# Attention's second head is asked for in the bias stage from four buffers; three smaller moves in the order of narrowing and of the last rows

## The chip, the cores and the metric

The kernel runs on one core of a Trainium2 chip. The metric is the device time of one execution in microseconds (us). Before the change three timed runs took 439.25, 441.69 and 442.11 us: 441.69 in the median. One more execution was profiled; its rows are those read here.

The engines are named as the profile names them: PE multiplies matrices (PEld is its loading of weights), DVE and ACT are the two vector engines, POOL is GpSimd, and SP only issues DMA transfers. Each works through its own list of instructions in order and waits on semaphores for the others. POOL and ACT can issue transfers too.

## The reference

Three layers, one after the other. Attention has 2 batches (B), 8 heads (H), 576 positions (S) and 64 numbers per head; its bias is made by a small net with 32 hidden units. A mixture of 8 experts follows, with at most 288 tokens for each, and a gated block on all 1152 tokens.

```
scores = scale * np.matmul(q, k.transpose(0, 1, 3, 2))
x = (psi_rel / psi_i)[..., None]
bias = np.maximum(x @ w1 + b1, 0.0) @ w2          # 576 x 576 for each head
scores = scores + bias.transpose(2, 0, 1)[None]
attn = softmax(scores);  out = np.matmul(attn, v)
...
h = relu(einsum("ecd,edf->ecf", disp, w1));  y = einsum("ecf,efd->ecd", h, w2)
...
g = x @ w_gate;  val = x @ w_val
return (g * sigmoid(g) * val) @ w_out
```

## The kernel before

Nearly every operand is split into a high part (a rounded copy) and a low part (what the copy left), and a product is made of two or three. The splitting is work for DVE, ACT and POOL.

**Bias stage** (`bias_phase`). 36 steps, each for 16 rows of positions. A step makes four tiles r of 128 x 576 (L587 on DVE; in seven of nine steps one of the four is L585 on ACT), multiplies them with w2 on PE (L591), copies the product out on ACT (`leave`, L600) and writes it to DRAM (biasd, L601) from one of six buffers (be). The bias tiles of head 0 are read back by `bias` (L196 to L202). Between the steps the rows of head 0 are split: they were asked for at the start, and ACT and DVE do it (`hi="A"`, `L=V`).

**Loads.** `loader` gives `load(h, b)`: a transfer of q, k and v of a head and a batch (raw, 800 KB, L227), then six instructions that make the split operands QK, K2 and W. The transfer is issued at the first step of this generator. For heads 1 to 7 all six are POOL's, in order L238 (twice), L240, L242, L247, L249. The buffers raw come from a pool of two.

**Attention stage** (`attn_phase`). 72 steps u, nine for each head. A step issues the scores of the next u (L296 on PE), the sum with the bias and the maximum (L311, DVE), the exponential (L328, ACT), the transposes (L348) and the split of what comes back (L351 ACT, L367 and L373 DVE), and pieces of older work on PE: the products with v (L395) and the products that gather the heads (L422). In head h the rows of head h+1 are asked for: at its steps 0 and 4 for head 0 (`LOADS0`), at 0 and 5 for the others (`LOADS`). `inv` (L409, nine elements for each of 128 partitions) prepares the division of a head. The order on each engine is the order in which this code is written.

**Experts** (`experts`, `Experts.full`). The routing is computed in four pieces (`route`). Expert by expert, eight weight blocks of 512 KB are loaded (wr, L999 and L1002), split (L1008 ACT, L1009 DVE) and used (L1038, L1052). Among them `extra(k)` puts one further piece at a time: the last piece of the routing (small, few, late), and for the gated block the narrowing of its 64-bit weights. `narrow(f)` is four steps: L790 and L792 on DVE, L794 on ACT, L796 on DVE, which then issues the load `load64(f + 2)`. `Y0` is how many places of the first expert pass before `extra(0)` begins.

**Gated block** (`swiglu`, `block`). Twelve steps f; each has two products (`gate(f, 0)` and `gate(f, 1)`, L1290 on PE, two tiles of 304 tokens), the elementwise part (L1297 ACT, L1298 DVE), the split of its result (`parts`, L1302 ACT, L1303 DVE) and the product with w_out of the step before (`outp`, L1311). In between stand the pieces of narrow(f + 3) and of split(f + 1). At the end five blocks of rows (t = 0 to 4) are copied out (L1319 ACT, L1321 DVE) and sent by POOL (`put`, L1322). `M2` and `M3` say how many of the products of the last but one step stand before the second half's gate and how many are left to the loop over the last blocks.

## Time and profile before

| | us |
|---|---|
| median of three timed runs | 441.69 |
| the profiled execution, its own time | 440.11 |
| its span, to which all rows refer | 437.9 |
| bias stage | 0 to about 66 |
| attention | about 66 to 219 |
| routing and first expert | about 219 to 269 |
| second and third expert | about 269 to 302 |
| gated block | about 302 to 438 |

Within the span PE is busy for 90%, DVE for 79%, ACT for 62% and POOL for 30%. A row of a timeline gives the start, the time, the engine, the line, the operation, the tiles (out<-in) and how many instructions are merged into it; in square brackets stands the idle time of the engine before it and what ended it. A merged row's time runs from the start of the first to the end of the last.

### The profile page before, as it was taken

The numbers are of one execution on the slowest core, as the hardware profiler recorded it, in microseconds if no ns is written. First come the engines' busy times: TensorE is split into PE (matmuls) and PEld (weight loads), VectorE is DVE, ScalarE is ACT, GpSimd is POOL, SyncE is SP. The second block draws the span as 40 slices with busy tenths as digits, with TensorE's granted clock in tenths as the row PEclk, the third lists the DMA queues.
The fourth block names the chain that finished last, engine by engine and source line by source line (L and its number), as shares of the span: only waits on it lengthen the run. The fifth ranks groups of instructions, "written<-read, shape, count | busy, mean of one in ns | idle before, by whom it ended". The sixth has DMA issues, their size and how long they took to land.

```text
span 437.9 us, 8781 instructions
## 1 busy us (share of the span) xinstructions
PE 395.4 (90%) x3136; PEld 344.2 (79%) x3136; DVE 345.7 (79%) x747; ACT 270.9 (62%) x579; POOL 131.2 (30%) x122
## 2 busy tenths in 40 slices
PE   8786678579999999999999989997979999999994
PEld 4332226579999999999989979995968888888992
DVE  6999996469999999999778878944887777777341
ACT  4888787469989899899624367444354444444221
POOL 2000000798979999995200300000000000000003
PEclk9999899889999999999999999999999999999998
DMA  7555447782766857732194898983444444440003
GB/s 255 210 217 191 162 190 237 260 293 82 226 184 206 258 166 236 239 99 77 28 283 137 230 293 188 335 229 129 145 144 145 144 146 144 145 144 2 0 1 117
DMA packets 54017, 75.75 MB, mean 173 GB/s; under 512 B 16514, under 2 KB 35714, under 8 KB 53968
## 3 DMA queue, kind: packets, MB, share of 16 engines
q1 hardware_dynamic: 51744, 70.62, 50.9%
q10 hardware_dynamic: 1616, 2.62, 2.1%
q0 software_dynamic: 608, 1.89, 1.3%
q8 instruction: 26, 0.43, 0.4%
q14 instruction: 23, 0.19, 0.2%
HBM read 58.54 MB, written 16.59 MB: 172 GB/s over the span
## 4 chain that ended last, share of the span: by engine, by line
PE 42%; DVE 21%; ACT 10%; DMA 7%; issue 6%; POOL 2%; SPq 1%; DVEq 0%; ACTq 0%; POOLq 0%
PE pg L1290 9%; PE tp L348 5%; PE po L395 5%; PE sc L296 5%; DMA wr<-in_ew 4%; DVE swl L806 4%; DVE wf L792 4%; PE ph L1038 4%; PE pb L591 3%; PE po L422 3%; ACT pth L351 2%; PE etp L910 2%; DVE sg L1298 2%; ACT ex L328 2%; DMA bias<-biasd 2%
## 5 line engine op out<-in xcount | busy, mean ns | idle before, releaser
L311 DVE CUSTOM_DVE_ANT_0 ex<-sc,bias 128x576 f32<-128x576 f32 x72 | 53.9, 750 | 9.7 <-PE tt L358 7.4
L591 PE MATMUL pb<-r,w 128*32 128x288 f32 x576 | 45.3, 424 | 15.1 <-ACT r L585 9.3
L238 POOL TENSOR_TENSOR QK<-raw,zero 128x640 fp32r<-128x640 f32 x28 | 34.5, 1253 | 78.0 <-DVE mx L311 75.4
L587 DVE TENSOR_SCALAR r<-ltab,sl,nb 128x576 f32<-128x576 f32 x116 | 57.3, 592 | 0.3 <-PE pb L591 0.2
L328 ACT ACTIVATE ex<-ex,mx 128x576 f32<-128x576 f32 x72 | 55.8, 775 | 1.4 <-DVE mx L311 0.7
L351 ACT ACTIVATE pth<-tp 128x512 fp32r<-128x512 f32 (+1 forms) x80 | 43.7, 553 | 16.3 <-PE tp L348 8.3
L296 PE MATMUL sc<-QK 128*128 128x288 f32 x160 | 49.6, 326 | 3.8 <-POOL QK L240 3.4
L591 PEld LDWEIGHTS pb<-r,w 128*32 128x32 f32 x576 | 18.6, 112 | 41.4 <-ACT r L585 21.7
L367 DVE TENSOR_TENSOR ptl<-tp,pth 128x512 fp32r<-128x512 f32 (+1 forms) x80 | 49.7, 629 | 1.7 <-ACT pth L351 1.0
L1290 PE MATMUL pg<-x2h,swh 128*128 128x304 f32 x192 | 46.4, 309 | 4.9 <-DVE sg L1298 4.1
L348 PE MATMUL tp<-cst,ex 128*128 128x128 f32 x288 | 45.1, 280 | 5.3 <-DVE ptl L367 3.1
L1322 POOL DMA_INDIRECT out<-ob,ids x5 | 4.9, 973 | 146.3 <-ACT ob L1319 145.4
L296 PE MATMUL sc<-K,QK 128*128 128x288 f32 x160 | 45.4, 299 | 1.2 <-POOL K L242 1.2
L1290 PE MATMUL pg<-x2l,swh 128*128 128x304 f32 x192 | 43.9, 303 | 0.0
L395 PE MATMUL po<-pth,W 128*128 128x256 f32 (+1 forms) x145 | 43.7, 322 | 0.0
L1290 PE MATMUL pg<-x2h,swl 128*128 128x304 f32 x192 | 43.6, 301 | 0.0
L348 PEld LDWEIGHTS tp<-cst,ex 128*128 128x128 f32 x288 | 33.1, 143 | 9.9 <-ACT ex L328 4.6
L1302 ACT ACTIVATE sh<-sg 128x608 fp32r<-128x608 f32 (+1 forms) x13 | 8.8, 673 | 51.1 <-DVE sg L1298 51.1
L1290 PEld LDWEIGHTS pg<-x2h,swh 128*128 128x128 f32 x192 | 32.7, 188 | 9.7 <-DVE sg L1298 7.1
L1298 DVE TENSOR_TENSOR sg<-pg,sg 128x304 f32<-128x304 f32 x48 | 20.7, 469 | 22.1 <-PE pg L1290 18.7
L296 PEld LDWEIGHTS sc<-QK 128*128 128x128 f32 x160 | 30.6, 191 | 5.5 <-POOL QK L240 3.6
L395 PE MATMUL po<-ptl,W 128*128 128x256 f32 (+1 forms) x116 | 33.4, 309 | 0.0
(209 smaller groups left out, 1041.9 us busy)
## 6 DMA issues: line engine op xcount, KB each, us to landing
raw<-in_qkv SPq DMA_DIRECT2D x16, 800.0 KB, 7.2
biasd<-be SPq DMA_DIRECT2D x36, 288.0 KB, 2.1
wr<-in_ew SPq DMA_DIRECT2D x19, 512.0 KB, 9.0
w<-in_mwg SPq DMA_DIRECT2D x12, 512.0 KB, 3.6
w<-in_mwv SPq DMA_DIRECT2D x12, 512.0 KB, 4.9
w<-in_mwo SPq DMA_DIRECT2D x12, 512.0 KB, 6.6
bias<-biasd SPq DMA_DIRECT2D x16, 288.0 KB, 4.0
bias<-biasd SPq DMA_DIRECT2D x17, 256.0 KB, 4.2
```

The costliest lines, as they stand in the source:

```text
L238: P.tensor_tensor(QK[:, o:o + n], raw[:, o:o + n], view(zero, 0, (0, n)), op=ALU.add)
L296: nc.tensor.matmul(sc[:, c, :288], l, K[:, o + c * 288:o + (c + 1) * 288], start=n == 0, stop=n == len(lhs) - 1)
L311: V.tensor_tensor_reduce(e.rearrange("p (c j) -> p c j", c=2), sc[:, :, :288], head[h][:, t].rearrange("p (c j) -> p c j", c=2), scale=-0.125,
L328: A.activation(ex[u], ex[u], AF.Exp, bias=mx, scale=-1.0, accum_out=sums[h][:, col:col + 1])
L348: nc.tensor.transpose(x[:, kt], e[:, kt * 128:(kt + 1) * 128], ident)
L351: A.activation(hi[:, :4, c], x[:, :, o], AF.Copy)
L367: V.tensor_tensor(lo[:, :, c], x[:, :, o], hi[:, :4, c].bitcast(F32), op=ALU.subtract)
L395: nc.tensor.matmul(po[:, :w], W[:, kt], src[:, kt, a:a + w], start=k == 0, stop=k == 8)
L587: V.tensor_scalar(r[g], x, s, nb, op0=ALU.mult, op1=ALU.max)
L591: nc.tensor.matmul(pb[strips[g], c, :288], w2, r[g][:, c * 288:(c + 1) * 288], start=True, stop=True, skip_group_check=True,)
L1290: nc.tensor.matmul(g[:, :TB], w[:, a * 4 + kk], x[:, kk, c0 + b * TB:c0 + (b + 1) * TB], start=kk == 0 and i == 0, stop=kk == 3 and i == 2,)
L1298: V.tensor_tensor(sg[:, cs], g[:, :TB], sg[:, cs], op=ALU.mult)
```

## The change

Four things. (1) The transfers of head 1 (both batches) are issued in the bias stage, at its steps 12 and 16, instead of at attention's steps 0 and 4, and the pool for raw has four buffers instead of two. The staging tiles of `prepare` lie in the bias stage's own pool. (2) `Y0` is 4 instead of 3. (3) In the gated block's step 1 the last step of narrow(3) comes after `parts` instead of before the older product. (4) `M3` is 3 instead of 1. The gated block's code is built three more times for other numbers of kept tokens, in branches that this execution does not enter.

```diff
--- before.py
+++ after.py
@@ -46,9 +46,11 @@
 
 ONA = (1, 2, 3, 5, 6, 7, 8)
 L0, L1 = 20, 2
+LOADS0 = (12, 16)
 STEPS1 = 4
 
-LOADS0, LOADS = (0, 4), (0, 5)
+RAW = 4
+LOADS = (0, 5)
 SHARE, SHARE4 = 0.68, 0.0
 LAST = (2.0, 2.0, 2.0, 2.0)
 LATE = ((7, 0, 1), (7, 1, 0), (7, 1, 1))
@@ -57,11 +59,11 @@
 NSPL = 3
 Q1 = 3
 N2 = 3
-Y0, Y1 = 3, 5
+Y0, Y1 = 4, 5
 REGS, LATE_REGS = 2, 5
 PICK = 3
 
-M2, M3 = 2, 1
+M2, M3 = 2, 3
 
 WARM0 = 7
 WARM = (16, 24)
@@ -214,7 +216,7 @@
 def loader(tc, ctx, ins):
 
     nc = tc.nc
-    raw_p = ctx.enter_context(tc.tile_pool(name="araw", bufs=2))
+    raw_p = ctx.enter_context(tc.tile_pool(name="araw", bufs=RAW))
     qk_p = ctx.enter_context(tc.tile_pool(name="aqk", bufs=4))
     V, A, P = nc.vector, nc.scalar, nc.gpsimd
     one = ctx.enter_context(tc.tile_pool(name="az", bufs=1))
@@ -454,9 +456,8 @@
         u += 1
         if u < nu:
             h, b, t = seq[u]
-            at = LOADS if h else LOADS0
-            if h + 1 < H and u % 9 in at:
-                b = at.index(u % 9)
+            if 0 < h < H - 1 and u % 9 in LOADS:
+                b = LOADS.index(u % 9)
                 loads.append(load(h + 1, b))
                 qk[h + 1, b] = next(loads[-1])
             if h + 1 < H and 1 <= u % 9 <= NQ:
@@ -506,9 +507,9 @@
     return late[0]
 
 
-def prepare(nc, pool, ins, rt, tids):
-
-    zi = pool.tile([128, DM], F32, name="zi")
+def prepare(nc, pool, one, ins, rt, tids):
+
+    zi = one.tile([128, DM], F32, name="zi")
     nc.gpsimd.memset(zi, 0.0)
     zb = pool.tile([128, 12], F32, name="zb")
     nc.gpsimd.memset(zb, float(BIG))
@@ -545,7 +546,7 @@
     for b in range(B):
         loads.append(load(0, b, "A", V))
         qk[0, b] = next(loads[-1])
-    others = prepare(nc, one, ins, rt, tids)
+    others = prepare(nc, pool, one, ins, rt, tids)
     zi = next(others)
 
     warm = ps.tile([128, 512], F32, name="pb1", tag="T")
@@ -612,6 +613,10 @@
             bias(0, k // 8 - 1)
         if k in (20, 21, 22):
             next(others, None)
+        if k in LOADS0:
+            b = LOADS0.index(k)
+            loads.append(load(1, b))
+            qk[1, b] = next(loads[-1])
         if k >= L0 and (k - L0) % L1 == 0:
             next(loads[0], None)
             if STEPS1 > (k - L0) // L1:
@@ -1351,7 +1356,11 @@
             elif f == 1:
                 for _ in split(2, (0, 1)):
                     pass
-            for _ in nar if f else ():
+            if f == 1:
+
+                for _ in range(2):
+                    next(nar, None)
+            for _ in nar if f > 1 else ():
                 pass
             if f:
                 outp(f - 1, *prev, 0, mid)
@@ -1359,7 +1368,7 @@
             if f == 0:
                 po = banks("po", range(nt))
             parts(sg, sh, sl, 0, nb)
-            for _ in () if f else nar:
+            for _ in () if f > 1 else nar:
                 pass
             if f:
                 outp(f - 1, *prev, mid, nt)
```

On SP's queue, in the bias stage: rows of the kernel before (biasd are the writes of bias tiles, bias the reads of head 0's, raw the rows of a head).

```order
L601 DMA biasd_91<-be 128x576 x2
L202 DMA bias<-biasd_90 128x576
L601 DMA biasd_91<-be 128x576 x6
L601 DMA biasd_92<-be 128x576 x2
L199 DMA bias<-biasd_91 128x512
L200 DMA bias<-biasd_91 128x64
```

The same place now.

```order
L602 DMA biasd_91<-be 128x576 x2
L204 DMA bias<-biasd_90 128x576
L602 DMA biasd_91<-be 128x576 x2
L229 DMA raw<-in_qkv 128x1600
L602 DMA biasd_91<-be 128x576 x4
L229 DMA raw<-in_qkv 128x1600
L602 DMA biasd_92<-be 128x576 x2
L201 DMA bias<-biasd_91 128x512
```

Two transfers of rows stand between the writes; they stood behind the whole stage before. On POOL the order is unchanged: head 1's instructions are the first behind its memsets.

On DVE, in the first expert, behind the routing's small instructions (late is their last; wf and w are the narrowing, wl the split of an expert's weights, hl that of its hidden tiles): before.

```order
L754 CAST late<-small 1x3
L790 TENSOR_SCALAR wf_3175<-w_3178 128x1536
L1009 TENSOR_TENSOR wl_3204<-wr_3197,wh_3203 128x1024
L874 TENSOR_LOAD regs x2
L1413 BRANCH_PREFETCH_HINT
L1043 SCALAR_TENSOR_TENSOR hl<-ph,hh 128x288
L792 SCALAR_TENSOR_TENSOR wf_3175<-w_3178,wf_3175 128x1536
L1043 SCALAR_TENSOR_TENSOR hl<-ph,hh 128x288
L1009 TENSOR_TENSOR wl_3206<-wr_3198,wh_3205 128x1024
L1043 SCALAR_TENSOR_TENSOR hl<-ph,hh 128x288
L796 SCALAR_TENSOR_TENSOR wf_3175<-w_3178,wf_3175 128x1536
```

The same place now.

```order
L1014 TENSOR_TENSOR wl_3204<-wr_3197,wh_3203 128x1024
L879 TENSOR_LOAD regs x2
L1422 BRANCH_PREFETCH_HINT
L1048 SCALAR_TENSOR_TENSOR hl<-ph,hh 128x288
L748 TENSOR_TENSOR small<-list 128x2
...
L759 CAST late<-small 1x3
L795 TENSOR_SCALAR wf_3175<-w_3178 128x1536
L1048 SCALAR_TENSOR_TENSOR hl<-ph,hh 128x288
L797 SCALAR_TENSOR_TENSOR wf_3175<-w_3178,wf_3175 128x1536
L1014 TENSOR_TENSOR wl_3206<-wr_3198,wh_3205 128x1024
```

One split of weights (wl_3204) now stands ahead of the routing's last piece and of the narrowing.

On DVE, in the gated block's step 1 (swl is the split of its weights, sg the elementwise part, sl the split of the result): before.

```order
L806 TENSOR_TENSOR swl_3181<-wf_3177,swh_3180 128x512 x2
L792 SCALAR_TENSOR_TENSOR wf_4279<-w_3179,wf_4279 128x1536
L796 SCALAR_TENSOR_TENSOR wf_4279<-w_3179,wf_4279 128x1536
L1298 TENSOR_TENSOR sg<-pg,sg 128x304 x2
L1303 TENSOR_TENSOR sl<-sg,sh 128x608
```

The same place now.

```order
L811 TENSOR_TENSOR swl_3181<-wf_3177,swh_3180 128x512 x2
L797 SCALAR_TENSOR_TENSOR wf_4279<-w_3179,wf_4279 128x1536
L1303 TENSOR_TENSOR sg<-pg,sg 128x304 x2
L1308 TENSOR_TENSOR sl<-sg,sh 128x608
L801 SCALAR_TENSOR_TENSOR wf_4279<-w_3179,wf_4279 128x1536
```

The last narrowing instruction (L796, now L801) moved behind the elementwise part and the split.

## Rows read from the trace of the kernel before

**Rows 1.** Page, part 1: busy us, share of the span and instructions, whole span

```profile
PE 395.4 (90%) x3136; PEld 344.2 (79%) x3136; DVE 345.7 (79%) x747; ACT 270.9 (62%) x579; POOL 131.2 (30%) x122
```

**Rows 2.** Timeline of DVE in the bias stage: start, us, line, tiles, count

```profile
11.74 32.91 DVE L587 TENSOR_SCALAR r<-ltab,sl,nb 128x576 f32<-128x576 f32 x67
```

**Rows 3.** Table of stretches, one head: length, busy PE PEld DVE ACT POOL, PEclk, DMA

```profile
124.40:141.60 17.20, 17.14 (x137) 16.45 (x137) 16.19 (x43) 15.72 (x45) 16.65 (x16) 1.00 0.58 175
```

**Rows 4.** Timeline of SP's queue: eight bias writes, first rows of head 1

```profile
24.77 11.14 SPq L601 DMA_DIRECT2D biasd<-be  x8
...
73.39 0.43 SPq L227 DMA_DIRECT2D raw<-in_qkv  x1
```

**Rows 5.** Timeline of POOL, head 1: first and last row of twelve instructions

```profile
78.72 2.46 POOL L238 TENSOR_TENSOR QK<-raw,zero 128x640 fp32r<-128x640 f32 x2 [75.42 <-DVE mx L311]
...
92.46 0.87 POOL L249 TENSOR_TENSOR W<-raw,W 128x320 fp32r<-128x320 f32 x1
```

**Rows 6.** Timeline of PE, first scores of head 1

```profile
82.84 0.40 PE L296 MATMUL sc<-QK 128*128 128x288 f32 x1 [3.37 <-POOL QK L240]
```

**Rows 7.** Timeline of DVE, first bias sum of heads 1, 2 and 3

```profile
88.35 0.76 DVE L311 CUSTOM_DVE_ANT_0 ex<-sc,bias 128x576 f32<-128x576 f32 x1 [7.15 <-PE tt L358]
...
108.06 0.75 DVE L311 CUSTOM_DVE_ANT_0 ex<-sc,bias 128x576 f32<-128x576 f32 x1
...
125.27 0.75 DVE L311 CUSTOM_DVE_ANT_0 ex<-sc,bias 128x576 f32<-128x576 f32 x1
```

**Rows 8.** Timeline of PE in the first expert: its three waits

```profile
256.45 0.40 PE L1052 MATMUL py<-hh,wl 128*128 128x288 f32 x1 [0.67 <-DVE wl L1009]
...
260.10 0.40 PE L1052 MATMUL py<-hh,wh 128*128 128x288 f32 x1 [0.33 <-ACT wh L1008]
261.36 0.40 PE L1052 MATMUL py<-hh,wl 128*128 128x288 f32 x1 [0.86 <-DVE wl L1009]
```

**Rows 9.** Timeline of PE in the gated block, step 2

```profile
321.04 0.41 PE L1290 MATMUL pg<-x2h,swh 128*128 128x304 f32 x1 [1.09 <-DVE sg L1298]
```

**Rows 10.** Page, part 6, DMA issues: count, KB, median us to landing

```profile
raw<-in_qkv SPq DMA_DIRECT2D x16, 800.0 KB, 7.2
```

**Rows 11.** Instructions of L409, in two stretches: ns min/median/max, first and last start

```profile
L409 DVE TENSOR_TENSOR rs<-sum,eps x1: 831/831/831, 147.0 to 147.0; 128x9 f32<-128x9 f32 x1
...
L409 DVE TENSOR_TENSOR rs<-sum,eps x1: 168/168/168, 164.4 to 164.4; 128x9 f32<-128x9 f32 x1
```

**Rows 12.** Timeline of POOL at these two places

```profile
146.89 0.87 POOL L249 TENSOR_TENSOR W<-raw,W 128x320 fp32r<-128x320 f32 x1
...
164.47 0.87 POOL L249 TENSOR_TENSOR W<-raw,W 128x320 fp32r<-128x320 f32 x1
```

**Rows 13.** Timeline of DVE in the first expert: two narrowing instructions

```profile
248.43 0.96 DVE L790 TENSOR_SCALAR wf<-w 128x1536 int32<-128x1536 int32 x1
...
250.81 1.75 DVE L792 SCALAR_TENSOR_TENSOR wf<-w,wf 128x1536 int32<-128x1536 int32 x1
```

**Rows 14.** Timeline of POOL in the first expert: gathers, their descriptor work

```profile
246.93 0.97 POOL L945 DMA_INDIRECT xh<-rows,ri  x1 [0.30 <-ACT wh L1008]
248.20 1.30 POOL L945 DMA_INDIRECT xr<-rows,ri  x1 [0.30 <-issue]
```

**Rows 15.** Timeline of ACT in the first expert

```profile
252.59 1.60 ACT L794 ACTIVATE w<-w 128x1536 f32<-128x1536 f32 x1 [2.33 <-DVE wf L792]
```

**Rows 16.** Timeline of DVE in the gated block, step 1

```profile
318.84 1.76 DVE L796 SCALAR_TENSOR_TENSOR wf<-w,wf 128x1536 int32<-128x1536 int32 x1 [1.68 <-ACT w L794]
320.51 0.85 DVE L1298 TENSOR_TENSOR sg<-pg,sg 128x304 f32<-128x304 f32 x2
```

**Rows 17.** Timeline of POOL at the end: third and fourth block sent

```profile
430.47 0.97 POOL L1322 DMA_INDIRECT out<-ob,ids  x1 [2.12 <-ACT ob L1319]
431.74 0.97 POOL L1322 DMA_INDIRECT out<-ob,ids  x1 [0.30 <-issue]
```

**Rows 18.** Page, part 5: L587, count, busy us, mean ns, idle before

```profile
L587 DVE TENSOR_SCALAR r<-ltab,sl,nb 128x576 f32<-128x576 f32 x116 | 57.3, 592 | 0.3 <-PE pb L591 0.2
```

## The prediction

> **What bounds the kernel now.** I read the busy shares of the page first [rows 1]: PE is nearly full over the span, but that is a mean over stages with different limits, so I went on to the table of stretches and the timelines, stage by stage.
>
> In the bias stage (to about 66 us) the DVE sets the pace. Its timeline has 67 of the products of L587 in one unbroken run of 32.91 us, 0.491 us each [rows 2]; the reader is to see that no idle time stands inside the run, so whatever holds the DVE there delays the end of the stage by as much. POOL does nothing in this stage.
>
> In the attention stage PE is full once it runs (17.14 of 17.20 us in one head's stretch [rows 3]), but between head 0 and head 1 everything stops. The rows of head 1 are asked for only at 73.39 us, when the bias stage is over [rows 4]; POOL starts to narrow them at 78.72 [rows 5]; PE waits for POOL at 82.84 [rows 6], and the DVE sits idle for 7.15 us before its first row of head 1 at 88.35 [rows 7]. Head 1 then takes 108.06 - 88.35 = 19.71 us to the first row of head 2, where the next head takes 125.27 - 108.06 = 17.21 [rows 7]. So the late start costs 7.15 + 2.50 = 9.65 us.
>
> In the first expert PE waits three times for split weights, 0.67 + 0.33 + 0.86 = 1.86 us [rows 8]. In the last stage PE waits 1.09 us for the DVE at 321.04 [rows 9]. The kernel ends with POOL sending the last blocks of rows.
>
> **The change part by part.** The sum is made against the profiled execution's own 440.11 us (span 437.9); the median of the three timed runs is 441.69, so 1.6 above it.
>
> *Head 1's rows early, the gain.* The two transfers move to the bias stage, behind the writes of tiles 11 and 15. In the run of eight writes that starts at 24.77 and takes 11.14 us [rows 4], 1.4 us each, these are the 2nd and the 6th: the rows are asked for at about 27.5 and 33, and land 7.2 us later [rows 10], at about 35 and 40. Four buffers mean that neither waits for one. On SP each costs about 0.4 us of issuing, between writes that wait for ACT anyway. Behind them in the queue stand writes of bias tiles, whose six staging buffers cover 6 x 1.4 = 8.4 us, more than the 7.2 of a transfer; if that cover went, ACT would be held by a microsecond or so. POOL's program has nothing in front of head 1's twelve instructions but memsets, so it narrows as soon as the rows land, 30 us before they are wanted. Head 1's stall is then gone: 9.65 us, of which the lower bound is 7.15, the wait by itself, if the slower head 1 has another cause. I take 9.65, since PE and DVE run the next head's same work in 17.21. Next late would be head 2's rows; with four buffers they no longer wait for POOL to leave a buffer, so they come earlier too.
>
> *The same step, its cost.* POOL's twelve instructions, from 78.72 to 92.46 + 0.87 = 93.33 us [rows 5], are 14.6 us of work. Beside attention they cost nothing. Now they fall into the unbroken run of the DVE. No row of before shows POOL arithmetic beside L587, so I bound the price. Nearest rows: the reciprocal's sum L409, nine elements with both inputs in SBUF, takes 0.168 us when it starts at 164.4, just before a POOL instruction (164.47), and 0.831 us when it starts at 147.0 inside one that ends at 146.89 + 0.87 = 147.76 [rows 11, 12]; it ends some 0.07 after it. So a DVE instruction can be held until the running POOL instruction is over. L587 has one tensor input, but it works at the double rate: L790 does 1536 elements in 0.96 us, L792 as many in 1.75 [rows 13]. If the one runs at twice the rate of the other and the rest of an instruction is alike, the 0.79 between them is half of the slower one's element time: 1.04 ns an element at the single rate, 0.52 at the double (estimates from these two rows). 576 elements would need 0.60 us at the single rate and L587 comes every 0.491, so it is at the double one. And the one place where such an instruction meets POOL shows friction on POOL's side: the descriptor work that starts at 248.20, under L790, took 1.30 us where the one before took 0.97 [rows 14]. Below, the cost could be nothing. Above, it is the whole 14.6. If POOL's instructions and the DVE's take turns, the DVE loses each POOL instruction less the part of its own 0.491 that isn't element work (0.491 - 576 x 0.52 ns = 0.19): 14.6 - 12 x 0.19 = **12.3 us**. I take this, since L409 is the nearest row and both its rows agree with it. Behind the waiting L587 stand PE's bias products, ACT's copies and SP's writes, all paced by the DVE, so the stage ends 12.3 us later and attention starts later by that.
>
> The Trainium skill ("SBUF — State Buffer", Who interferes with whom) says that tensor_scalar between SBUF tiles can take a two-port mode, that it and a GpSimd instruction then exclude each other for a whole instruction, and that one outside these modes with a single SBUF input doesn't meet GpSimd at all. No run here yet shows L587 beside POOL; by its first half the sum stands as above, by its second the loss would be zero, the first rival.
>
> *Route and narrowing one step later (Y0).* The eleven small instructions and the narrowing of the first gate block move behind one split of weights, and ACT's long w (1.60 us at 252.59 [rows 15]) moves behind the split that PE waits for. The three waits go: 1.86 us, with a lower bound of 0 if the later splits are caught by the same instructions. One weight load goes out ahead of the three loads of the gate block; that block is wanted only in the second expert. I take 1.86.
>
> *One step of the third narrowing later.* L796 no longer stands between 318.84 and the products at 320.51 [rows 16], so PE's 1.09 at 321.04 [rows 9] goes. But the DVE has to do it before the next step's products, and PE waits there too. Between 0 and 1.09; no row decides, I take 0.5. The load behind it goes out some 2 us later and has a whole step to land.
>
> *Last rows (M3).* The same products in another order; three fewer stand in front of the third block of rows, but it waits for its inputs instead. POOL sends the last three blocks every 1.27 us (430.47, 431.74 [rows 17]), and that chain starts where it did. Between -0.2 and +0.7 (three products), I take 0.
>
> Sum: 12.3 - 9.65 - 1.86 - 0.5 = +0.3 us: **440.4** against its own 440.1, 442.0 by the median. I write 441.0, between the two. What the stall gives back, the DVE pays in the bias stage.
>
> **The rivals.**
>
> *The narrowing is hidden.* POOL runs beside L587 without holding it, or is itself held until attention starts (then its 14.6 us start at 66 instead of 78.72 and still come in time). For it: in attention POOL is busy 16.65 of 17.20 us [rows 3] and the DVE keeps its pace, and L790 kept its 0.96 us under POOL's descriptor work. Against it: L409. Loss 0: -9.65 - 1.86 - 0.5 = -12.0, so 428.1 by its own time, 429.7 by the median.
>
> *A hand-over costs more than the instruction.* L587's instructions overlap: 0.491 apart, yet 0.592 long [rows 2, 18]. If each of twelve hand-overs lets one of them in at its full length and POOL keeps the rest, the loss is 14.6 + 12 x 0.10 = 15.8, net +3.8: 443.9, or 445.5 by the median. For it: both rows of L409 show the hold to the very end. Against it: the DVE's start-up can lie under the hold. Over 1% slower from a loss of 16.4 on.
>
> *It doesn't do what it says*: the page names a DVE instruction (mx) as what ended POOL's long idle time before head 1. If POOL really waits for attention's first rows, there is neither loss nor most of the delay, which is the hidden case again; only if the rows landed as late as now would the step bring nothing and cost nothing, and -2.4 remain, 437.7. SP has room, so I give it little.
>
> **How the numbers follow.** Forecast (loss 10 to 14.6): 0.55, own range 437 to 446. Hidden: 0.29. Costly hand-over: 0.13. Rows late: 0.03. One per cent is 4.4 us, about what a measurement can tell here. Faster by over 1%: the hidden case, 0.29, and the part of the forecast with a loss under 8, 0.09: 0.38. Slower: 0.10 of the hand-over and 0.07 of the forecast where the expert's 1.86 doesn't come or head 1 gives back only 7.15: 0.17. Within: 0.45. The range must reach to the hidden case: 428 to 446, with one in ten below and under one in ten above.
>
> **What would show it.** In the new profile POOL's twelve instructions lie at about 35 to 60 us. Right: there the DVE's unbroken run has instructions of over 1 us, and the stage ends near 78; the first row of head 1 follows that of head 0 after about 13.5 us without a long idle time, and head 1 takes 17.2. The PE rows at 256 to 262 have no waits. Wrong: the DVE's run stays at 0.491 and attention starts at 66 (hidden), or POOL's instructions are longer than before while the DVE's are not (POOL is the one that is held), or head 1 still stalls.

## The result, and the profile after

| | before | after |
|---|---|---|
| median of four runs, us | 441.90 (439.25 to 442.77) | 446.35 (445.57 to 446.98) |
| after / before | | 1.0107, 95% interval 1.0061 to 1.0153 |
| span of the profiled execution, us | 437.9 | 443.7 |

The change makes the kernel 1.1% slower. The forecast was 441.0 with a range up to 446.0, so the time lies just above the range, on the side that had a chance of 0.17.

The page of after, the shares of part 1 and the granted clock of part 2 (40 equal slices, about 11.1 us each):

```profile
PE 398.9 (90%) x3136; PEld 343.3 (77%) x3136; DVE 355.4 (80%) x747; ACT 270.8 (61%) x579; POOL 142.2 (32%) x122
...
PEclk9998758999999999999999999999998999999998
```

The counts are those of [rows 1], but the DVE is busy 9.7 us longer and POOL 11.0 us longer: the same instructions last longer somewhere. PE's clock is lower in the 5th and 6th slice (7 and 5; before has 8 and 9 there), where PE waits more. The timelines say for what. (In after the lines stand one to five further down: L587 is L588, L238 is L240, L311 is L313, L1290 is L1295.)

POOL in after, head 1's rows (start, us, line, tiles, count, idle time before); four of ten rows:

```profile
34.79 11.51 POOL L240 TENSOR_TENSOR QK<-raw,zero 128x640 fp32r<-128x640 f32 x2 [31.48 <-DMA raw<-in_qkv]
46.38 1.66 POOL L242 TENSOR_TENSOR QK<-raw,QK 64x640 fp32r<-64x640 f32 x1
...
52.38 2.89 POOL L240 TENSOR_TENSOR QK<-raw,zero 128x640 fp32r<-128x640 f32 x2
...
59.66 0.96 POOL L251 TENSOR_TENSOR W<-raw,W 128x320 fp32r<-128x320 f32 x1
```

The twelve instructions lie at 34.8 to 60.6 us, as promised. But the first two, 2.46 us of work in [rows 5], take 11.51.

The DVE in the same stretch:

```profile
7.43 36.33 DVE L588 TENSOR_SCALAR r<-ltab,sl,nb 128x576 f32<-128x576 f32 x74
44.08 4.27 DVE L588 TENSOR_SCALAR r<-ltab,sl,nb 128x576 f32<-128x576 f32 x3 [0.32 <-PE pb L592]
48.38 3.31 DVE L242 TENSOR_TENSOR QK<-raw,QK 64x640 fp32r<-64x640 f32 x2
51.73 8.17 DVE L588 TENSOR_SCALAR r<-ltab,sl,nb 128x576 f32<-128x576 f32 x6
59.82 2.22 DVE L244 TENSOR_TENSOR K<-raw,QK 128x640 fp32r<-128x640 f32 x2
61.96 6.45 DVE L588 TENSOR_SCALAR r<-ltab,sl,nb 128x576 f32<-128x576 f32 x13
```

The reader is to see two regimes. Up to 43.76 the products come every 0.491 us (36.33 / 74) although POOL has had its rows since 34.8: POOL is the one that waits. Then the DVE has its first gap, 0.32 us for PE, and 46.30 - 2.46 = 43.84: POOL gets in there, or a little before, as the two may not follow without a break. From then on they take turns, the six products of the fourth row take 1.36 us each, and behind 61.96 all is as before.

The last products of the stage, before and after:

```profile
57.77 7.93 DVE L587 TENSOR_SCALAR r<-ltab,sl,nb 128x576 f32<-128x576 f32 x16
```

```profile
68.73 7.92 DVE L588 TENSOR_SCALAR r<-ltab,sl,nb 128x576 f32<-128x576 f32 x16
```

They end at 65.70 and at 76.65, 10.95 us apart. The first product of the stage starts at 4.89 before and at 5.47 after; two versions below with the same early rows start at 4.78 and 4.83, so this is not the change's. So the hold itself is 10.95 - 0.58 = 10.4 us.

The first bias sum of head 0 in before ([rows 7] has those of heads 1 to 3), then of heads 0 to 3 in after:

```profile
67.80 0.76 DVE L311 CUSTOM_DVE_ANT_0 ex<-sc,bias 128x576 f32<-128x576 f32 x1 [2.09 <-ACT be L600]
```

```profile
79.67 0.76 DVE L313 CUSTOM_DVE_ANT_0 ex<-sc,bias 128x576 f32<-128x576 f32 x1 [3.00 <-ACT W L247]
...
93.61 0.76 DVE L313 CUSTOM_DVE_ANT_0 ex<-sc,bias 128x576 f32<-128x576 f32 x1 [0.59 <-PE tt L360]
...
113.26 0.75 DVE L313 CUSTOM_DVE_ANT_0 ex<-sc,bias 128x576 f32<-128x576 f32 x1
...
130.46 0.75 DVE L313 CUSTOM_DVE_ANT_0 ex<-sc,bias 128x576 f32<-128x576 f32 x1
```

Head 0 starts 11.87 us later: the 10.4 of the hold, the 0.58 at the start of the stage, and 0.9 more of waiting between the last product and the first sum (3.00 instead of 2.09). The idle 7.15 us are gone, yet from head 1 to head 2 it is 113.26 - 93.61 = 19.65 us, as long as before.

PE's waits in after at the three places that the moves touch later on (small expert's last weights, second step of the gated block, last rows):

```profile
304.70 0.64 PE L1095 MATMUL py<-wr,hs 128*32 128x128 f32 x16 [1.88 <-DMA wr<-in_ew]
...
331.63 0.41 PE L1295 MATMUL pg<-x2h,swh 128*128 128x304 f32 x1 [1.91 <-DVE sg L1303]
...
433.74 0.51 PE L1316 MATMUL po<-swh,sh 128*128 128x512 f32 x1 [0.36 <-ACT sh L1307]
```

In the first expert PE waits for nothing between 250 and 262 us any more, and the 1.09 of [rows 9] is gone too. These three have come instead.

How far after lies behind before, at the same instruction of both (starts from the timelines):

| instruction | before | after | behind by | this step |
|---|---|---|---|---|
| first bias sum of head 0 | 67.80 | 79.67 | 11.87 | +11.87 |
| first of head 1 | 88.35 | 93.61 | 5.26 | -6.61 |
| first of head 2 | 108.06 | 113.26 | 5.20 | -0.06 |
| last of head 7 | 209.18 | 214.74 | 5.56 | +0.36 |
| split of the first expert's result (x2l) | 270.38 | 273.86 | 3.48 | -2.08 |
| split of the second expert's (x2l) | 293.44 | 296.13 | 2.69 | -0.79 |
| split of the small expert's (x2l) | 302.17 | 306.42 | 4.25 | +1.56 |
| gate product (sg) of the gated block, second step | 331.24 | 336.53 | 5.29 | +1.04 |
| last gate product | 427.52 | 432.73 | 5.21 | -0.08 |
| end of the span | 437.9 | 443.7 | 5.8 | +0.6 |

The table compares one execution of each kernel. They are 5.8 us apart where the medians are 4.45 apart, and the timed runs of before alone spread over 3.5 us, so a step of about a microsecond needs an experiment before it is the change's.

### The profile page after: what moved, and what is told of

Read it like the earlier page. It is cut to its first block, busy times and chain, and to the rows that moved or that the text cites. A ratio compares the mean times of both kernels' runs of the same rounds, so it can differ in the third digit from the quotient of the medians.

```text
span 443.7 us, 8786 instructions
## 1 busy us (share of the span) xinstructions
PE 398.9 (90%) x3136; PEld 343.3 (77%) x3136; DVE 355.4 (80%) x747; ACT 270.8 (61%) x579; POOL 142.2 (32%) x122
## 5 line engine op out<-in xcount | busy, mean ns | idle before, releaser
L592 PE MATMUL pb<-r,w 128*32 128x288 f32 x576 | 50.9, 466 | 21.1 <-DVE r L588 12.0
L240 POOL TENSOR_TENSOR QK<-raw,zero 128x640 fp32r<-128x640 f32 x28 | 44.0, 1592 | 70.1 <-ACT pth L364 35.6
L588 DVE TENSOR_SCALAR r<-ltab,sl,nb 128x576 f32<-128x576 f32 x116 | 65.1, 646 | 0.4 <-PE pb L592 0.3
L313 DVE CUSTOM_DVE_ANT_0 ex<-sc,bias 128x576 f32<-128x576 f32 x72 | 53.9, 749 | 4.1 <-ACT W L247 3.0
L1295 PE MATMUL pg<-x2h,swh 128*128 128x304 f32 x192 | 46.6, 311 | 4.8 <-DVE sg L1303 3.8
L350 PE MATMUL tp<-cst,ex 128*128 128x128 f32 x288 | 44.1, 276 | 5.2 <-DVE ptl L369 3.5
L1295 PE MATMUL pg<-x2l,swh 128*128 128x304 f32 x192 | 44.4, 306 | 0.0
L1295 PE MATMUL pg<-x2h,swl 128*128 128x304 f32 x192 | 44.3, 306 | 0.0
L397 PE MATMUL po<-pth,W 128*128 128x256 f32 (+1 forms) x145 | 42.8, 317 | 0.0
L1295 PEld LDWEIGHTS pg<-x2h,swh 128*128 128x128 f32 x192 | 33.2, 191 | 9.3 <-DVE sg L1303 6.5
L601 ACT ACTIVATE be<-pb,kap 128x576 f32<-128x576 f32 x36 | 26.6, 738 | 22.3 <-issue 9.7
```

Source lines behind the costliest of these rows:

```text
L240: P.tensor_tensor(QK[:, o:o + n], raw[:, o:o + n], view(zero, 0, (0, n)), op=ALU.add)
L313: V.tensor_tensor_reduce(e.rearrange("p (c j) -> p c j", c=2), sc[:, :, :288], head[h][:, t].rearrange("p (c j) -> p c j", c=2), scale=-0.125,
L350: nc.tensor.transpose(x[:, kt], e[:, kt * 128:(kt + 1) * 128], ident)
L397: nc.tensor.matmul(po[:, :w], W[:, kt], src[:, kt, a:a + w], start=k == 0, stop=k == 8)
L588: V.tensor_scalar(r[g], x, s, nb, op0=ALU.mult, op1=ALU.max)
L592: nc.tensor.matmul(pb[strips[g], c, :288], w2, r[g][:, c * 288:(c + 1) * 288], start=True, stop=True, skip_group_check=True,)
```

## The experiments

Ratios are to runs of the kernel before that were timed beside each version, with a 95% interval.

**The first part alone.** Against the changed kernel, with the third narrowing back in its old place too:

```diff
-Y0, Y1 = 4, 5
+Y0, Y1 = 3, 5
-M2, M3 = 2, 3
+M2, M3 = 2, 1
```

> The first part of the change alone (head 1's rows among the bias tiles, four buffers); the three moves are undone. Theory now (POOL's twelve instructions and the DVE's products take turns; head 1 keeps its slow row): the bias stage ends near 76.5 us, some 11.8 us late; head 1's first row comes 13.9 us after head 0's instead of 20.55, and head 1 still takes 19.7; net +5.2 us, near 445.3 for the profiled execution against 440.1 before. Rival (the forecast's step as it was written, 9.65 us back): +2.6, near 442.7. Rival (the three moves are what made it slower): +0 or faster, 441 or less.

Measured: 1.0101 (1.0061 to 1.0141), span 443.9. The last bias product ends at 77.2, head 0 starts at 80.16, head 1 at 93.82 (13.7 us later), head 2 at 113.50 (19.7 later). The first part alone makes the whole slowdown; the forecast's step (+2.6) is not what it does. Here the run of products ends at 45.66 without idle time, and POOL gets in all the same: its first instruction, 1.23 us of work, ends at 46.77, so it begins near 45.5, where the first of head 0's subtractions follows the products. That subtraction takes 1.76 us (before, two take 1.56). POOL, then the DVE:

```profile
35.31 11.46 POOL L240 TENSOR_TENSOR QK<-raw,zero 128x640 fp32r<-128x640 f32 x1 [32.01 <-DMA raw<-in_qkv]
```

```profile
45.70 1.76 DVE L242 TENSOR_TENSOR QK<-raw,QK 64x640 fp32r<-64x640 f32 x1
```

The stage takes 71.27 us from its first product to the end of its last (5.91 to 77.18), 71.18 in after, 60.81 in before.

**The three moves alone.** Against the kernel before, with the third narrowing as in after:

```diff
-Y0, Y1 = 3, 5
+Y0, Y1 = 4, 5
-M2, M3 = 2, 1
+M2, M3 = 2, 3
```

> The three moves without the first part. Theory now, by the ledger of the two traces: the first expert gains about 2 us, of which 1.6 are lost again at the last weights of the second expert (PE waits 1.9 us there instead of 0.3); the narrowing moved in the last stage costs 1.0 (PE waits 1.9 us at the second step, and the clock falls behind it); the last rows cost 0.3 to 0.6. Net about +1, near 441. Rival (the forecast's terms): -1.86 - 0.5 + 0, near 437.7. If the wait for the last weights stays at 0.3 us here, the wait in the changed kernel came from the shift of the stages and not from the move.

Measured: 1.0014 (0.9977 to 1.0050), span 442.0. No difference that can be measured, against the forecast's -2.4 us. The first expert gains (its split comes 1.9 us earlier, counted from the last bias sum of head 7), but PE then stands 3.2 us at the small expert's last weights:

```profile
301.73 0.64 PE L1090 MATMUL py<-wr,hs 128*32 128x128 f32 x16 [3.21 <-DMA wr<-in_ew]
```

SP asks for the weights behind the first expert 2.77 us after that expert's split in every one of these kernels, so what is gained up to the split is kept. The last of these weights land 28.1 us after the ask in after (276.63 to 304.70), in the first part alone and with the earlier due date below; 27.3 in before, 29.4 here. So what PE gains behind the ask, it waits: from the first expert's split to the second's it is 22.27 us with the move (here and in after) and 23.06 in before. But the wait is not the move's alone. Without the move PE waits 0.3 us there in before, 1.1 in the first part alone, 1.3 and 1.1 in the next two below and 1.8 with the strided table further down; with it 1.9 in after. It does not come from the shift of the stages either: here nothing is shifted. Why the landing takes 27.3 us once and 29.4 another time stays open.

Here the clock falls behind the wait as well, and from the small expert's split to the first gate product it is 6.79 us where before has 4.51 and after 4.58. In the table of stretches (columns as in [rows 3]), over the nine microseconds behind the wait:

```profile
301.70:310.70 9.00, 7.73 (x48) 7.20 (x49) 1.91 (x4) 3.86 (x7) 0.00 (x0) 0.62 0.04 1
```

**POOL held until the bias stage is over**, the first part otherwise unchanged: head 1's rows are added to a zero of their own, which the DVE writes behind its last product.

```diff
+    gate = one.tile([128, 1], F32, name="gate")
...
+        z = gate if h == 1 else zero
...
-                P.tensor_tensor(QK[:, o:o + n], raw[:, o:o + n], view(zero, 0, (0, n)), op=ALU.add)
+                P.tensor_tensor(QK[:, o:o + n], raw[:, o:o + n], view(z, 0, (0, n)), op=ALU.add)
...
+    V.memset(load.gate, 0.0)
     leave(S // 16 - 1, pb)
```

> The first part alone, with one thing more: POOL adds head 1's rows to a zero that the DVE writes behind its last product of the bias stage, so the transfers are as early as in the change but POOL narrows only afterwards. Theory (POOL's arithmetic beside the DVE's double-rate products is the loss): the products keep 0.491 us, the bias stage ends near 65.6 as before, POOL narrows from about 66 to 81, head 1's first row comes 13.9 us after head 0's; net -6.7, near 433.4. Rival (the transfers among the bias tiles hold SP, ACT or the DMA engines, and POOL only happens to be there): the bias stage still ends near 76, net +5. Rival (POOL, starting at 66, is too late or slows the DVE in attention): head 1's first row comes 16 us or more after head 0's, net -4 or less gain.

Measured: 0.9848 (0.9826 to 0.9870), span 432.9. The last product ends at 65.3; the transfers are where they were in the run above, so neither they nor SP nor ACT held the stage: POOL's arithmetic did. Not all as expected: head 1 starts 83.12 - 67.48 = 15.64 us after head 0, not 13.9. The rows show why; first POOL, then the DVE:

```profile
65.38 2.46 POOL L242 TENSOR_TENSOR QK<-raw,gate 128x640 fp32r<-128x640 f32 x2 [62.08 <-DVE nil L280]
67.92 1.55 POOL L244 TENSOR_TENSOR QK<-raw,QK 64x640 fp32r<-64x640 f32 x1
69.55 1.68 POOL L246 TENSOR_TENSOR K<-raw,QK 128x640 fp32r<-128x640 f32 x1
```

```profile
68.17 1.66 DVE L253 TENSOR_TENSOR W<-raw,W 128x320 fp32r<-128x320 f32 x1
```

Head 0's last subtraction on the DVE takes 1.66 us where the one that after does at 68.33, beside an idle POOL, takes 0.48: with both inputs in SBUF it is held by L244, and one of attention's first rows is late by as much.

**One due date in attention**, on the kernel before. In head 0 the products of rows 256 to 575 of batch 0 with the values are due one row earlier.

```diff
-    work += [(6, pv(0, 0, 0)), (8, pv(0, 1, 0)), (11, pv(0, 0, 1)), (13, pv(0, 1, 1))]
+    work += [(6, pv(0, 0, 0)), (8, pv(0, 1, 0)), (10, pv(0, 0, 1)), (13, pv(0, 1, 1))]
```

> The kernel before with one number changed: the third group of value products of head 0 (rows 256 to 575 of batch 0) is due at row 10 instead of 11. Theory: head 1's slow row (4.15 us from its fourth to its fifth row, against 1.9 elsewhere) is ACT waiting to overwrite the one pth buffer of batch 0, which those products still read; with the products one row earlier, ACT's wait of 2.86 us shrinks to well under 1 and head 1 takes 17.5 us instead of 19.71; net -2, near 438. Rival (head 1 is slow because its rows came late, as the forecast has it): head 1 still takes 19.7, net 0.

Measured: 0.9941 (0.9918 to 0.9965), span 437.0. Head 1 takes 106.35 - 88.85 = 17.50 us instead of 19.71. ACT writes the turned rows of batch 0 into one buffer (pth0), from which these products still read. Before, and with the earlier due date:

```profile
96.09 0.60 ACT L351 ACTIVATE pth<-tp 128x512 fp32r<-128x512 f32 x1 [2.86 <-PE po L395]
```

```profile
94.13 0.60 ACT L351 ACTIVATE pth<-tp 128x512 fp32r<-128x512 f32 x1 [0.72 <-PE po L395]
```

These 2.21 are nearly all of the 2.50 us that the forecast laid to the late start of head 1. They have nothing to do with when the rows arrive: in after, where the rows are early, head 1 takes 19.65. In this execution 0.8 us of the gain is lost ahead of head 1, which starts 21.38 us after head 0 instead of 20.55.

**Is it the double rate? First try: a strided table.** Two kernels, the one before and the first part alone, in which the products read their table with a stride of two elements (two copies fill it).

```diff
-    ltab = pool.tile([128, 1148], F32, name="ltab")
+    ltab = pool.tile([128, 1148, 2], F32, name="ltab")[:, :, 0]
```

> The kernel before with the table of the bias products read with a stride of two elements (two copies of 1.2 us in all make it), so that the products cannot run at the double rate; nothing else changed. By the forecast's own estimate (0.19 us plus 576 x 1.04 ns) each product comes every 0.79 us instead of 0.491; 116 of them make the bias stage 35 us longer, to about 100 us. It stands beside the next run. If the products keep 0.49 us, the stride does not change the rate and the pair tells nothing.

> The same slower products, with head 1's rows among the bias tiles (the first part of the change alone) and POOL narrowing them beside the products. Theory (what excludes POOL is the products' double rate): POOL narrows at its own pace, twelve instructions in about 14.6 us with no long wait, the products keep their pace and the bias stage ends where it does in the run beside it, within 1 us. Rival (any DVE instruction on this memory and POOL's hold each other): POOL waits for a gap again and the stage ends some 11 us later than in the run beside it. Rival (both run and share the memory's rate): no stretch without POOL, but products and POOL instructions both longer, by 10 to 50%.

Measured (one profile each): spans 446.2 and 449.4. The stride changes nothing in the pace, 39.43 / 80 = 0.493 us:

```profile
7.66 39.43 DVE L590 TENSOR_SCALAR r<-ltab,sl,nb 128x576 f32<-128x576 f32 x80
```

So the pair says nothing of the rate. It does repeat the loss: the last product ends at 67.88 without POOL beside it and at 78.49 with it, 10.6 us.

**Second try: another form of the same product.** Again the kernel before and the first part alone; the maximum is taken with a column in PSUM by an instruction of two tensor inputs, one in SBUF and one in PSUM.

```diff
+    V.tensor_copy(pk[:, 8:9], nb)
...
-                V.tensor_scalar(r[g], x, s, nb, op0=ALU.mult, op1=ALU.max)
+                V.scalar_tensor_tensor(r[g], x, s, view(pk, 8, (0, S)), op0=ALU.mult, op1=ALU.max)
```

> The kernel before with another form for the bias products on the DVE: the same product and maximum as a scalar_tensor_tensor whose second operand is the same column kept in PSUM, so one input is in SBUF and one in PSUM. Estimate from the forecast's two rows (single rate 1.04 ns an element): 0.79 us each instead of 0.491, the bias stage some 35 us longer, to about 100 us. It stands beside the next run; if the products still come every 0.49 us, the form is no slower.

> The same slower form, with head 1's rows among the bias tiles and POOL narrowing them beside it (the first part of the change alone). Theory (the hold belongs to the double-rate form of the products): POOL's twelve instructions take about 14.6 us from the landing of the rows, without the long first wait, and the bias stage ends within 1 us of the run beside it. Rival (POOL's arithmetic holds any DVE instruction that reads or writes this memory): the stage ends 10 us or more later than in the run beside it, with POOL's first two instructions waiting again. Between: 1 to 10 us.

Measured (one profile each): spans 469.7 and 464.2. The DVE's long run without and with POOL, and POOL's first row beside it:

```profile
10.24 55.91 DVE L588 SCALAR_TENSOR_TENSOR r<-ltab,sl,pk 128x576 f32<-128x576 f32 x77 [0.36 <-ACT kap L609]
```

```profile
10.87 55.91 DVE L589 SCALAR_TENSOR_TENSOR r<-ltab,sl,pk 128x576 f32<-128x576 f32 x77 [0.36 <-ACT kap L610]
```

```profile
44.38 2.46 POOL L240 TENSOR_TENSOR QK<-raw,zero 128x640 fp32r<-128x640 f32 x2 [41.08 <-DVE r L589]
```

The products now come every 0.726 us (0.79 was estimated), and the run is 55.91 us long in both, though POOL's twelve instructions (44.38 to 60.74) lie in it; these have their lengths of [rows 5]. The last product ends at 95.11 without and at 95.74 with POOL, and the run began 0.63 later: loss 0. With the hold gone, the early rows bring their gain: head 1 starts 13.33 us after head 0 instead of 20.15, and the span is 5.5 us shorter. Instruction, rate and the place of an input change together here, so the pair shows that the hold belongs to the products' old form, and not which of the three matters. The Trainium skill ("SBUF — State Buffer", Who interferes with whom) says that a DVE instruction outside the two-port modes with at most one input in SBUF does not meet GpSimd; these rows agree.

**More of POOL's work.** The first part alone, eight of the twelve instructions issued twice.

```diff
+                for _ in range(1 + (h == 1)):
                     P.tensor_tensor(QK[:, o:o + n], raw[:, o:o + n], view(zero, 0, (0, n)), op=ALU.add)
```

(and the same around the subtraction for K).

> The first part alone, with eight of head 1's twelve narrowing instructions issued twice, which adds 2 x (2.46 + 1.55) = 8.0 us of work to POOL's 14.6 (the second issue writes the same values). Theory (turns: the DVE loses each POOL instruction less 0.19 us of its own): the bias stage ends 8.0 - 8 x 0.19 = 6.5 us later than with the twelve alone, near 83.5. Rival (the loss is a fixed price of the meeting, or of the fallen clock): it ends near 77 as with the twelve. Rival (POOL only takes what the DVE leaves once the first twelve are done): between the two.

Measured (one profile): the last product ends at 83.02, 5.8 us after that of the twelve alone (77.18), where turns gave 6.5; from the stage's first product on it is 6.2. The loss grows with POOL's work, and nearly at the rate of the forecast's formula; it is no fixed price. POOL's first row is again long, 16.27 us for 4.9 us of work: it ends at 51.46, and the first of its four instructions at 46.44, so POOL got in near 45.2, where the DVE's first run gives way to a subtraction (45.36) without a gap. POOL, then the DVE (the run up to 45.32):

```profile
35.19 16.27 POOL L241 TENSOR_TENSOR QK<-raw,zero 128x640 fp32r<-128x640 f32 x4 [31.88 <-DVE r L590]
```

```profile
7.51 37.81 DVE L590 TENSOR_SCALAR r<-ltab,sl,nb 128x576 f32<-128x576 f32 x77
```

**Versions that should beat both.** First, the rounding of head 1's rows by ACT in the bias stage (six activations), POOL's six subtractions held until the stage is over, and the earlier due date.

```diff
+            for o, n in ((0, SQ), (SQ, SK)):
+                A.activation(QK[:, o:o + n], raw[:, o:o + n], AF.Copy)
```

> A version that should beat both: the rows among the bias tiles; the rounding of head 1's rows done by ACT in the bias stage (six activations, some 4 us, in its idle time); the six subtractions left to POOL (8.2 us), held behind the DVE's last product by a write of the DVE into the tile they fill; and the third group of value products due at row 10. The three moves are undone. Theory: products at 0.491 us, bias stage ends near 65.5; POOL subtracts from 65.5 to 74, so head 1's first row comes 13.9 us after head 0's (15.64 where POOL did all of it) and head 1 takes 17.5 us; -6.6 - 2.2 = -8.8, near 431.3 for the profiled execution. Rival (ACT has no room): the bias stage ends up to 4 us later and the net is -5.

Measured: 0.9846 (0.9788 to 0.9904), span 434.6. ACT has not the room: the products end at 66.4, but the DVE then waits 3.99 us for ACT, and attention begins at 70.41. No better than POOL held, though it has the earlier due date on top.

Second, let go late: all narrowing by POOL, held until the DVE writes a zero behind the second row of attention, so that head 0's last subtraction is free too; with the earlier due date. The memset of the held version stands in the loader instead:

```diff
+        if h == 1 and b == 0:
+            V.memset(gate, 0.0)
```

> A version that should beat both: the rows among the bias tiles; POOL does all the narrowing but is held until the DVE has written a zero behind the second row of attention, so that neither the bias products nor head 0's last subtraction (held 1.66 us instead of 0.49 where POOL was let go at the stage's end) meets it; the third group of value products due at row 10; the three moves undone. Theory: bias stage ends near 65.3, POOL narrows from about 69 to 84, head 1's first row 13.9 to 14.3 us after head 0's and head 1 17.5 us: -6.4 - 2.2 = -8.6, near 431.5 for the profiled execution, ratio about 0.98. Rival (POOL is now too late): head 1's fifth row, the first of batch 1, waits for POOL, and the gain is that of the version let go at the stage's end, -5 - 2.2 = -7.2, near 432.9.

Third, the same with the route one step later (Y0 4 instead of 3).

> The same with the route and narrowing one step later in the first expert (the first of the three moves). Theory (transfers bound the way to the small expert's last weights): the three waits of 1.86 us go, but PE waits 1.9 to 3.2 us for the last weights instead of 1.1 to 1.3; net -1 to +0.4 against the run beside it, a ratio between the two within 0.3%. Rival (the forecast's term): -1.86, a ratio of 0.996.

Measured: 0.9792 (0.9756 to 0.9828) and 0.9801 (0.9761 to 0.9841), spans 432.4 and 431.2. Both beat the kernel before by 2% and, by their ratios, the changed one by 3%; between the two no difference can be measured. The moved route does bring 1.6 us up to the first expert's split here (59.36 us from the last bias sum of head 7 instead of 60.92), but behind the small expert's last weights, where PE waits 1.78 us instead of 1.26, the clock is 0.62 instead of 0.81 and the way to the first gate product 1.0 us longer. The second version's profiled execution is 434.3, not the 431.5 expected. POOL starts at 70.74 and is done at 85.5; head 1 starts 82.09 - 68.78 = 13.31 us after head 0 and takes 18.1:

```profile
70.74 2.46 POOL L244 TENSOR_TENSOR QK<-raw,gate 128x640 fp32r<-128x640 f32 x2 [67.43 <-DVE gate L238]
```

```profile
82.09 0.76 DVE L318 CUSTOM_DVE_ANT_0 ex<-sc,bias 128x576 f32<-128x576 f32 x1 [0.59 <-PE tt L365]
```

The rival (POOL too late) does not hold: the DVE's wait there is 0.59 us, and for PE.

## Why the prediction was wrong

**POOL holds the DVE (12.3): right in the mechanism, 1.9 too dear.** The hold is 10.4 us in after and in the first part alone. Attention starts 11.87 us later (12.4 in the first part alone), which is nearer to 12.3 by luck: 0.58 of it is the later start of the stage and 0.9 the longer wait behind it. The mechanism is shown from three sides: with POOL held the loss is gone, with more POOL work it grows, with another form of the product it is gone too. The step rested on L409 [rows 11, 12], and that reading stood. The double rate worked out from [rows 13] fits the slower pace of the other form (0.726 measured, 0.79 estimated), but no run changes the rate by itself. The hidden case (0.29), for which the free DVE in attention spoke [rows 3], does not happen. The costlier hand-over (15.8) does not either.

What the step didn't foresee is that POOL waits first, 9 us in after, to the first gap in the DVE's run of products, and 10 us in the first part alone, where no gap comes and it gets in where a subtraction follows the products. The forecast had it narrow from 35 us on at its own pace. It changed nothing in the sum, as the stage was long enough for all twelve instructions afterwards. A stage of products alone, without gap and without subtraction, was not tried.

**Head 1's stall (9.65): the step that failed.** The 7.15 us of idle time went, and 6.61 of them were gained. The other 2.50, "since PE and DVE run the next head's same work in 17.21", did not come: head 1 takes 19.65. The comparison of head 1 with head 2 [rows 7] was taken for the cost of a late start, and the row inside head 1 that is long was passed over. That row was in the trace of before: ACT's wait of 2.86 us, until 96.09, for products of PE; the due date shows that it is for a buffer, and takes head 1 to 17.50. The forecast named 7.15 as the lower bound, "if the slower head 1 has another cause", and should have taken it; the sum would then have been +2.8.

**Route and narrowing later (1.86): nearly there on the way, nothing in the time.** The three waits of [rows 8] are gone. From the last bias sum of head 7 to the first expert's split it is 59.1 to 59.4 us in the three kernels with the move (after, the three moves alone, the last version) and 60.7 to 61.2 in before and in the ten other versions: about 1.5 us come. Of the 1.56 that the table has given back at the small expert's last weights, half is not the move's: from the first expert's split to the small expert's it is 31.79 us in the one execution of before, but 32.4 to 33.2 in the ten others without the move, and 32.56 in after. The other half, 0.79, is gained behind the ask for the weights and waited at their landing. The forecast said that one weight load goes out ahead of the others and looked at the gate block alone, not at the next place where PE waits for a transfer, nor at the clock, which fell behind that wait in two of the three kernels with the move (and in some without). By the timed runs the moves are worth nothing that can be measured.

**Third narrowing (0.5): the size right without the clock, lost with it.** The wait of 1.09 goes [rows 9], and as the forecast said, the DVE pays at the next step: 1.91 instead of 1.10. In the three moves alone the two steps together take 17.32 us (317.07 to 334.39) against 17.88 before (313.36 to 331.24), a gain of 0.56. In after the same two steps take 18.85 (317.68 to 336.53): PE's clock falls behind the same 1.91 us of waiting. The table of stretches, columns as in [rows 3], in after and in the three moves alone:

```profile
330.00:335.00 5.00, 3.37 (x15) 3.37 (x16) 3.63 (x5) 1.62 (x1) 0.00 (x0) 0.71 0.61 193
```

```profile
330.00:335.00 5.00, 3.98 (x26) 3.85 (x27) 3.62 (x6) 1.01 (x1) 0.00 (x0) 1.00 0.51 171
```

A mean of 0.71 lies between the two levels, 2.4 GHz and 1.2: PE does 15 products instead of 26, and the two steps are 1.5 us longer.

**Last rows (0): on the dear side.** PE stops 0.36 us for ACT at 433.74, and from the last gate product to the end of the span it is 11.0 us in after and 11.3 in the three moves alone, against 10.4 in before [rows 17]. So +0.6 to +0.9, around the upper bound of 0.7.

By the table of steps the misses nearly all point one way: 2.98 (head 1) + 0.36 (later heads) + 0.55 (experts) + 1.54 (narrowing and clock) + 0.52 (last rows) - 0.43 (POOL's hold) = 5.5, and the span is 5.8 us longer where the sum gave 0.3. Of the first, 2.44 is the wrong reading of head 1, the largest miss with one cause, and 0.54 the 0.59 us that the DVE still waits for PE. The -0.43 is -1.9 of the hold against +1.5 around it. The others come of costing each small edit at the wait that it removes, and of comparing two single executions.

## What to carry to other kernels

A slow stretch behind a stall need not be the stall's: before it goes into the gain, find the row in it that is long and what that row waits for. Work put on GpSimd beside a stream of the DVE's fast single-input form can cost the DVE most of its own length (here 10.4 us for 14.6); let it wait on something that the DVE writes when the stream is over, and the transfer can still be early. And a wait removed from PE is a gain only until PE next waits for a transfer that was asked for before the gain.

## What the runs showed of the hardware

Which of the two is held depends on who is in. A stream of products without a gap kept POOL out for 9 us in after and 10 us in the first part alone, and lost nothing. From one gap of 0.32 us on, or from the first subtraction (two inputs in SBUF) on, the two took turns: 17 us for POOL's 14.6 us of work.

The stride of a tensor input (two elements) leaves the pace of the products as it is, 0.493 us against 0.491; the other instruction, with a second input in PSUM, makes it 0.726.

The clock does not fall at every stall of the same length. Over the nine microseconds that follow the small expert's last weights, the table of stretches gives 0.81 in the version let go late, where PE had waited 1.26 us, and 1.00 in the one held only to the end of the bias stage, where it had waited 1.30:

```profile
293.50:302.50 9.00, 7.72 (x54) 7.29 (x55) 2.80 (x6) 3.85 (x7) 0.00 (x0) 0.81 0.04 1
```

```profile
295.49:304.49 9.00, 7.76 (x65) 7.33 (x66) 4.10 (x6) 3.89 (x7) 0.00 (x0) 1.00 0.05 3
```

Nor does the longer wait decide: behind 1.88 us the clock is 1.00 over nine microseconds in after, behind 1.78 it is 0.62 in the last version. What decides was not found. From the small expert's split to the first gate product it is 6.03 us in the version let go late and 4.50 in the one held to the end of the stage, so a fall moves the span of a single profile by 1.5 us. This is one reason why the span of the version let go late is only 5.5 us under that of before while its runs are 2.1% faster; the other is that the profiled execution of before (440.11) is a quick one, as the runs timed beside this version have a median of 443.46.
